# Products with the identity in TensorE's gaps ahead of the first MLP stage, and an earlier gate for one pair of loads

## The chip, the cores and the metric

The kernel runs on one NeuronCore of a Trainium2 chip. Its engines are TensorE (PE, the matmuls), VectorE (DVE), ScalarE (ACT), GpSimd (POOL) and SyncE (SP), which issues most of the DMAs. Each works through a queue of its own, in order, and waits on semaphores for the others. The metric is the device time of one execution in microseconds (us); less is better.

## The reference

Attention with normalised q and k (8 batches, 12 heads, 448 positions, head size 64), followed by an MLP over the 3584 tokens (768 to 2048 to 768):

```python
q_n = q / (norm(q) + 1e-06);  k_n = k / (norm(k) + 1e-06)
scores = matmul(q_n, k_n.T) / tau                 # tau = 0.1
attn = softmax(scores)                            # over the keys
x = matmul(attn, v)                               # heads side by side: 3584 x 768
h = x @ w_in                                      # 768 x 2048
out = (h * cos(h)) @ w_out                        # 2048 x 768
```

Inputs and output are float32; inside, the matmuls are in bfloat16.

## The kernel before, in words

**Tiling.** A *quad* is four heads of one batch: three quads make a batch, 24 quads the whole. Quads are numbered from 0; buffers rotate (`Qf`, `Kf`, `qT`, `kT` three deep, so quad 5 uses slot 2 and quad 7 slot 1, which quad 4 leaves). The 448 positions are cut in NJ = 7 slices, so `scores(7 * quad + j)` makes one slice of keys against all queries.

**One quad.** SP loads q and k (`load_qk`, L391, 448 KB each), POOL issues the load of v (L403). The squares (`square`, L436 on ScalarE or L439 on POOL) are summed on DVE (L443); `inverse` turns the sums into factors with small Ln and Exp steps on ScalarE (L461, L473) and two DVE steps (L476, L479); `scale` multiplies (L500); `transpose` turns q and k on TensorE (L522) with a copy out of PSUM (L532 on DVE, L530 on ScalarE), or, for later quads, `turn` does it by DMA (L539). `scores` is four 64x64 matmuls (L557) and one Exp of 128x896 on ScalarE, called E (L564). `spread` (L596) sums E over the keys with a matrix of ones, `attend` (L574) multiplies E with v; `invert_spread` (L609, L613) and `scale_x` (L625, DVE) finish a part of x. Where scores are made, pairs of PSUM banks alternate: score g waits until an earlier E has left its bank.

**The MLP.** For each batch c there are two stages: first `m1_part` (L677, eight pairs of 448-column sums over six 128-row slices of x and W1) with h * cos(h) behind it on ScalarE and DVE (`m1`: L690, L692, L694, L696, the result gT); then `m2` (L705, gT with W2), cut into pieces between which the scores, spreads and attends of later quads stand. Outputs leave PSUM by a DVE copy (L714) and SP's stores (L727).

**The order.** The program is written out as a list of operations (`op`), with a key each. TensorE's order is that of the keys. Up to `P.strict = False` (L954) the other engines' queues follow the keys too, which are the numbers of the operations shifted by a table, `MOVE`; behind it the Planner orders those queues when the program is built, from estimated durations and due times (`pass_`). Quads 0 to 2 are done before the first MLP stage: this is the *head*.

**Products with the identity.** `warm(n, bank)` (L803) puts n matmuls of the 128x128 identity with itself on TensorE; nothing reads what they leave. The kernel has six such groups (40, 24, 5, 8, 5 and 20).

**The gate.** POOL issues the loads of W1 (L413) and of W2 in four parts (L418, `half[2]` is parts 1 and 2, `half[3]` parts 3 and 4). The two loads of quad 5 wait until W2's third part has landed:

```python
    load_qk(5, half[3][:1])                       # L905
    ...
    load_qk(FIRST + 3, half[3])                   # L955: quad 6, after parts 3 and 4
    ...
                turn(FIRST + 1, half[3])          # L979: quad 4's transposes, likewise
```

Quad 7's loads are issued by `begin(3)` (L757), behind L954.

Of the kernel before, what the change touches and what calls it, by code (L numbers as in the profile page):

```python
# [21 lines left out]
class Planner:  # L22
# [13 lines left out]
    def __init__(self):  # L36
        self.ops = []
        self.last_write = {}
        self.readers = {}
        self.strict = False  # L40
        self.tail = {}

    def op(self, eng, dur, fn, r=(), w=(), after=(), dma=None, moves=0, mode="f", chain=None, keep=False, lead=0.0,
           packet=74, lock=False):
        o = Op()
        o.i, o.eng, o.dur, o.fn, o.dma, o.moves, o.mode, o.chain = (
            len(self.ops), eng, dur, fn, dma, moves, mode, chain)
        o.lat = self.FIRST + moves + self.LAST if dma else self.LAT[eng]
        o.behind, o.lead, o.packet, o.lock = None, lead, packet, lock
        o.key = o.i + (self.MOVE.get(o.i, 0) if self.strict else 0)  # L50
        if keep or self.strict and eng in ("act", "dve", "pool", "sp"):
            self.tail.setdefault(eng, []).append(o)
        o.reads, o.writes = tuple(r), tuple(w)
        deps = {a.i for a in after if a is not None}
        for x in o.reads:
            if x in self.last_write:
                deps.add(self.last_write[x].i)
        for x in o.writes:
            if x in self.last_write:
                deps.add(self.last_write[x].i)  # L60
            deps.update(p.i for p in self.readers.get(x, ()))
        deps.discard(o.i)
        o.deps = sorted(deps)
        for x in o.reads:
            self.readers.setdefault(x, []).append(o)
        for x in o.writes:
            self.last_write[x] = o
            self.readers[x] = []
        self.ops.append(o)
        return o  # L70

    def land(self, ring, issued, took, packet):
        s = max(issued + self.FIRST, self.ring[ring][0])
        for other, (until, theirs) in self.ring.items():
# [13 lines left out]

    def plan(self):
        for line in self.tail.values():  # L90
            line.sort(key=lambda o: o.key)
            for a, b in zip(line, line[1:]):
                b.behind = a
        self.order = self.pass_([0.0] * len(self.ops))
        return self.order
# [172 lines left out]
def bass_cosine_attention__then__act_gcu_kernel(  # L268
# [28 lines left out]
    def sb(name, shape, dt):  # L297
        return ctx.enter_context(nc.sbuf_tensor(name, shape, dt))
# [28 lines left out]
    ident = sb("ident", [128, 128], BF16)  # L327
# [4 lines left out]
    def bank(i, n=S, p0=0, p1=128):  # L332
        return PS.ap()[p0:p1, 512 * i:512 * i + n]
# [4 lines left out]
    P = Planner()  # L338
    op = P.op
    X, Y = 4, 5  # L340

    iot = ar[2].ap()[:, 0, 0:128].bitcast(I32)
    op("pool", 0.3, lambda e: e.iota(iot, [[1, 128]], base=0, channel_multiplier=-1), w=[("ar", 2)])
    op("dve", 0.25, lambda e: e.tensor_scalar(ident.ap(), iot, 0, None, ALU.is_equal), r=[("ar", 2)], w=["ident"])

    def fill_sel(e):
# [3 lines left out]
        return e.memset(sel.ap()[64:128, 16:32], 1.0)  # L350

    op("dve", 0.3, fill_sel, w=["sel"])
    op("dve", 0.1, lambda e: e.memset(ones.ap(), 1.0), w=["ones"])
    for i in range(2):
        op("dve", 0.1, lambda e, i=i: e.memset(ne.ap()[:, i, :, 1], 1e-6), w=[("eps", i)])

    mode = [None]
# [18 lines left out]
    def cut(kind, u, part):  # L376

        return [(kind, u, i) for i, (j0, j1) in enumerate(HALVES) if part[0] < j1 and j0 < part[1]]

    def whole(bk):  # L380
        return cut("B", bk, ALL[0])
# [4 lines left out]
    def load_one(qd, w, part=ALL[0], after=()):  # L386
        b, h0, s = qd // QB, 2 * (qd % QB), qd % 3
        src, dst, nm = ((q, Qf, "Qf"), (k, Kf, "Kf"))[w]
        j0, j1 = part
        ap = bass.AP(src.tensor, (b * NH + h0) * S * D + j0 * D, [[NJ * D, 128], [NH // 2 * S * D, 2], [1, (j1 - j0) * D]])  # L390
        return op("sp", 0.6, lambda e: e.dma_start(dst[s].ap()[:, :, j0:j1].rearrange("p r j d -> p r (j d)"), ap),  # L391
                  w=cut(nm, s, part), dma=(nm, s, j0), moves=0.17 * (j1 - j0), after=after)

    def load_qk(qd, after=()):
        return [load_one(qd, w, after=after) for w in range(2)]
# [98 lines left out]
    def scale(qd, w, eng="pool", part=ALL[0]):  # L494
        s, u = qd % 3, qd % 2
        j0, j1 = part
        f, n, nm = ((Qf, Qn, "Q"), (Kf, Kn, "K"))[w]
        rb = bass.AP(rr, (2 * u + w) * H + j0, [[4 * H, 128], [NJ, 2], [1, j1 - j0], [0, D]])
        return op(eng, (1.05 if eng == "dve" else 1.65) * (j1 - j0) / NJ,
                  lambda e: e.tensor_tensor(n[0].ap()[:, j0:j1].rearrange("p j r d -> p r j d"), f[s].ap()[:, :, j0:j1],  # L500
                                            rb, ALU.mult),
                  r=cut(nm + "f", s, part) + cut("rr%d" % w, u, part), w=cut(nm + "n", 0, part), lock=True)
# [44 lines left out]
    def scores(g, bs=None):  # L547
        qd, j = divmod(g, NJ)
        assert holds.get(g % NE, 0) // NJ in summed or g < NE
        holds[g % NE] = g  # L550
        u, es = qd % 3, g % NE
        bs = 2 * (g % 2) if bs is None else bs

        def mm(e):
            for r in range(2):
                for a in range(2):
                    ins = e.matmul(bank(bs + r, S, 64 * a, 64 * a + 64),  # L557
                                   kT[u].ap()[64 * r:64 * r + 64, j, a, :],
                                   qT[u].ap()[64 * r:64 * r + 64, :, a, :],
                                   start=True, stop=True)  # L560
            return ins

        op("pe", 0.2, mm, r=cut("QT", u, ALL[0]) + cut("KT", u, (j, j + 1)), w=pair(bs), mode="q")
        act("exp", 0.81, lambda e: e.activation(E[es].ap(), two(bs), ACT.Exp, bias=0.0, scale=INV_TAU),  # L564
            r=pair(bs), w=[("E", es)], chain="E")
# [52 lines left out]
    def scale_x(qd, bk=None):  # L618
        b, c0, s = qd // QB, 2 * (qd % QB), qd % 3
        if bk is None:  # L620
            sl = qd % NA
            op("dve", 1.01, lambda e: e.tensor_tensor(xT[b % 2].ap()[:, c0:c0 + 2, :], AVs[sl].ap(), ar[s].ap(), ALU.mult),
               r=[("AV", sl), ("ar", s)], w=[("x", b % 2, qd % QB)], lead=LEAD, lock=True)
            return
        op("dve", 1.01, lambda e: e.tensor_tensor(xT[b % 2].ap()[:, c0:c0 + 2, :], two(bk), ar[s].ap(), ALU.mult),  # L625
           r=pair(bk) + [("ar", s)], w=[("x", b % 2, qd % QB)])
# [146 lines left out]
    def next_pair():  # L773
        turns[0] += 1
        return 2 * (turns[0] % SLOTS)
# [9 lines left out]
    def visit(slots):  # L785
        for kind, x in slots:
# [13 lines left out]
                begin(qd)  # L800
            scores(x, next_pair())

    def warm(n, bk=0):  # L803

        def mm(e):
            for _ in range(n):
                ins = e.matmul(bank(bk, 128), ident.ap(), ident.ap(), start=True, stop=True)
            return ins

        op("pe", (0.057 if bk else 0.08) * n, mm, r=["ident"], w=whole(bk), after=[P.ops[-1]] if n < 40 and bk == 0 else ())  # L810

    P.strict = True
    warm(40)
    first = load_one(0, 0)
    for part in HALVES:
# [4 lines left out]
    half = [[], []]  # L820
# [7 lines left out]
    adds = [square(0, 1, "act", part) for part in HALVES]  # L828
    add()
    warm(24)  # L830
    adds[0]()
    adds[1]()
# [3 lines left out]
    for _ in inverse(0, 1, 2, HALVES[1]):  # L836
        pass
    scale(0, 0, "dve")
    warm(5)
    scale(0, 1, "dve", HALVES[0])  # L840
    scale(0, 1, "dve", HALVES[1])
# [60 lines left out]
    transpose(2, 1, Z + 1, HALVES[0])  # L902
    scores(12)
    scaled = scale(2, 1, "dve", HALVES[1])
    load_qk(5, half[3][:1])  # L905
    scale_x(0, X)
    scores(13)
    transpose(2, 1, Z + 1, HALVES[1])
# [156 lines left out]
```

## Time and profile before

| | us |
|---|---|
| median of 3 runs | 424.02 |
| the three runs | 423.82, 424.02, 425.92 |
| the profiled execution, time | 424.78 |
| its span, from first to last instruction | 423.0 |
| start of the first MLP stage (first L677) | 35.99 |
| start of the second MLP stage | 90.60 |
| mean granted clock of TensorE | 0.996 |

| engine | busy us | share of the span |
|---|---|---|
| PE | 408.5 | 97% |
| ACT | 308.2 | 73% |
| DVE | 268.5 | 63% |
| POOL | 201.1 | 48% |

The profile is of one execution. A busy TensorE is not TensorE at its peak, since matmuls overlap in the records: a row's length holds the time in the pipe, and successive starts show the rate. The granted clock is a share of full speed (1.00 or, where it is held back, less). "Idle before", in square brackets, is how long an engine stood still and what ended it. The chain of waits follows the work that ended last back to the start. Times in the text are from the span's start.

### The profile page before, as it was taken

How to read it: one execution, taken by the hardware profiler on the slowest of the kernel's cores; microseconds unless marked ns; L12 is line 12 of the kernel's file. 1: busy time of each engine (PE TensorE's matmuls, PEld its weight loads, DVE VectorE, ACT ScalarE, POOL GpSimd, SP SyncE). 2: the span in 40 equal slices, each digit the busy share in tenths (PEclk: the TensorE clock that was granted, in tenths of full speed). 3: DMA queues.
4: the chain of work that ended last, by engine and by line, in shares of the span. 5: the costliest groups of instructions: out<-in, count | busy, mean ns of one | idle time of the engine just before them, and what ended most of it. 6: DMA issues, size and time to landing. Idle time of an engine off the chain costs nothing.

```text
span 423.0 us, 8505 instructions
## 1 busy us (share of the span) xinstructions
PE 408.5 (97%) x3586; PEld 214.0 (51%) x3586; DVE 268.5 (63%) x335; ACT 308.2 (73%) x406; POOL 201.1 (48%) x137
## 2 busy tenths in 40 slices
PE   6889998999999999999999999999999999999996
PEld 6344454445545445445554554454554555555563
DVE  4766786888954649753896459814783137826931
ACT  5898888997888977698778848689778557605700
POOL 1476437884287796659538963269403213000000
PEclk9899999999999999999999999999999999999999
DMA  8999998997089979687949992289705624021032
GB/s 272 247 241 210 235 220 154 237 202 178 2 186 178 288 155 265 87 172 161 218 126 206 181 247 60 42 153 218 162 0 82 133 63 94 2 74 39 1 76 74
DMA packets 71127, 62.83 MB, mean 149 GB/s; under 512 B 40496, under 2 KB 66096, under 8 KB 71088
## 3 DMA queue, kind: packets, MB, share of 16 engines
q1 hardware_dynamic: 60688, 50.28, 51.9%
q0 software_dynamic: 10240, 11.80, 16.9%
q8 instruction: 28, 0.46, 0.5%
q10 hardware_dynamic: 160, 0.20, 0.1%
q14 instruction: 11, 0.09, 0.1%
HBM read 45.61 MB, written 11.01 MB: 134 GB/s over the span
## 4 chain that ended last, share of the span: by engine, by line
PE 74%; DMA 12%; DVE 4%; POOL 4%; ACT 3%; SPq 2%; issue 1%; ACTq 0%; POOLq 0%
PE PS L705 29%; PE PS L677 27%; PE PS L557 7%; PE PS L574 6%; DMA W<-in_moe_w_out_dram 6%; DMA Kf<-in_k_dram 4%; PE PS L635 3%; DMA R<-Zs 2%; ACT E L564 1%; PE PS L596 1%; SPq L656 1%; POOL xT L659 1%; POOL sqq L439 1%; DVE gT L696 1%; DVE n L443 1%
## 5 line engine op out<-in xcount | busy, mean ns | idle before, releaser
L705 PE MATMUL PS<-W,gT 128*128 128x384 bf16 x896 | 156.7, 327 | 0.0
L564 ACT ACTIVATE E<-PS 128x896 bf16<-128x896 f32 x168 | 143.2, 917 | 17.7 <-PE PS L557 16.2
L677 PE MATMUL PS<-xT,W 128*128 128x448 bf16 x768 | 147.2, 353 | 1.0 <-POOL xT L659 0.5
L705 PEld LDWEIGHTS PS<-W,gT 128*128 128x128 bf16 x896 | 83.2, 98 | 69.2 <-issue 16.2
L677 PEld LDWEIGHTS PS<-xT,W 128*128 128x128 bf16 x768 | 74.5, 98 | 71.8 <-POOL xT L659 0.9
L690 ACT ACTIVATE ar<-PS 128x896 int32<-128x896 f32 x64 | 58.1, 911 | 41.8 <-PE PS L677 41.6
L692 DVE SCALAR_TENSOR_TENSOR ar<-ar,PS 128x896 f32<-128x896 int32 x64 | 69.1, 1084 | 22.6 <-ACT ar L690 22.6
L696 DVE TENSOR_TENSOR gT<-PS,ar 128x896 bf16<-128x896 f32 x64 | 69.4, 1088 | 7.8 <-ACT ar L694 7.4
L694 ACT ACTIVATE ar<-ar 128x896 f32<-128x896 f32 x64 | 60.5, 947 | 16.6 <-DVE ar L692 16.0
L714 DVE COPY osb<-PS 128x384 f32<-128x384 f32 x56 | 31.1, 556 | 60.6 <-PE PS L705 60.1
L439 POOL TENSOR_TENSOR sqq<-Qf 128x896 bf16<-128x896 f32 x22 | 36.9, 1677 | 42.9 <-DMA Qf<-in_q_dram 22.6
L659 POOL TENSOR_TENSOR xT<-AVs,R 128x896 bf16<-128x896 f32 x18 | 37.6, 2089 | 41.4 <-DMA R<-Zs 41.2
L557 PE MATMUL PS<-qT,kT 64*64 64x448 bf16 x672 | 49.2, 362 | 4.2 <-ACT E L564 3.1
L500 POOL TENSOR_TENSOR Qn<-Qf,rr 128x896 bf16<-128x896 f32 x21 | 38.1, 1812 | 27.9 <-DVE rr L479 24.8
L439 POOL TENSOR_TENSOR sqk<-Kf 128x896 bf16<-128x896 f32 x21 | 36.8, 1754 | 17.4 <-DVE n L443 14.6
L443 DVE TENSOR_REDUCE n<-sqq 128x14 f32<-128x896 bf16 x24 | 25.7, 1072 | 24.0 <-POOL sqq L439 20.2
L583 DVE COPY AVs<-PS 128x896 f32<-128x896 f32 x21 | 22.9, 1091 | 23.5 <-PE PS L574 23.4
L574 PE MATMUL PS<-E,Vb 64*64 64x448 bf16 x672 | 37.0, 351 | 0.3 <-DVE kT L532 0.3
L557 PEld LDWEIGHTS PS<-qT,kT 64*64 64x64 bf16 x672 | 16.5, 105 | 30.2 <-issue 12.2
L500 POOL TENSOR_TENSOR Kn<-Kf,rr 128x896 bf16<-128x896 f32 x18 | 30.4, 1687 | 1.9 <-DMA kT<-Kn 1.9
L443 DVE TENSOR_REDUCE n<-sqk 128x14 f32<-128x896 bf16 (+2 forms) x25 | 26.0, 1041 | 4.6 <-POOL sqk L439 3.6
L403 POOL DMA_DIRECT2D Vb<-in_v_dram x24 | 18.1, 755 | 18.0 <-PE PS L557 12.4
(47 smaller groups left out, 180.9 us busy)
## 6 DMA issues: line engine op xcount, KB each, us to landing
Qf<-in_q_dram SPq DMA_DIRECT2D x24, 448.0 KB, 5.3
out_dram<-osb SPq DMA_DIRECT2D x54, 192.0 KB, 3.4
Kf<-in_k_dram SPq DMA_DIRECT2D x23, 448.0 KB, 6.0
R<-Zs SPq DMA_DIRECT2D x72, 112.0 KB, 3.2
Vb<-in_v_dram POOLq DMA_DIRECT2D x24, 224.0 KB, 6.6
W<-in_moe_w_in_dram POOLq DMA_DIRECT2D x4, 768.0 KB, 18.4
W<-in_moe_w_out_dram POOLq DMA_DIRECT2D x4, 768.0 KB, 24.1
qT<-Qn SPq DMA_TRANSPOSE x20, 4.0
```

Source lines behind the costliest of these rows:

```text
L439: op(eng, (1.68 if eng == "pool" else 1.05) * n, lambda e: e.tensor_tensor(dst, src, src, ALU.mult), r=cut(nm + "f", s, part), w=cut("sq" ...
L443: return op("dve", 0.07 + 0.95 * n, lambda e: e.tensor_reduce(out=n2.ap()[:, u, H * w:H * w + H] if part == ALL[0] else jr(n2, u, w, part) ...
L500: lambda e: e.tensor_tensor(n[0].ap()[:, j0:j1].rearrange("p j r d -> p r j d"), f[s].ap()[:, :, j0:j1], rb, ALU.mult),
L557: ins = e.matmul(bank(bs + r, S, 64 * a, 64 * a + 64), kT[u].ap()[64 * r:64 * r + 64, j, a, :], qT[u].ap()[64 * r:64 * r + 64, :, a, :], s ...
L564: act("exp", 0.81, lambda e: e.activation(E[es].ap(), two(bs), ACT.Exp, bias=0.0, scale=INV_TAU), r=pair(bs), w=[("E", es)], chain="E")
L574: ins = e.matmul(bank(bk + a, S, 64 * r, 64 * r + 64), Vb[vs].ap()[64 * a:64 * a + 64, r, j, :], E[es].ap()[64 * a:64 * a + 64, r, :], sta ...
L677: ins = e.matmul(bank(bk + i2), W1.ap()[:, i, 128 * nb:128 * nb + 128], xT[c % 2].ap()[:, i, :], start=(i == 0), stop=(i == NKC - 1))
L690: op("act", 0.815, lambda e: e.activation(ar[s].ap().bitcast(I32), two(bk), ACT.Identity, bias=0.25, scale=INV2PI), r=bs, w=[("ar", s)])
L692: op("dve", 1.005, lambda e: e.scalar_tensor_tensor(ar[s].ap(), ar[s].ap().bitcast(I32), -2.0 * math.pi, two(bk), ALU.mult, ALU.add), r=bs ...
L694: act("sin", 0.86, lambda e: e.activation(ar[s].ap(), ar[s].ap(), ACT.Sin, bias=GUARD * math.pi / 2.0, scale=GUARD), r=[("ar", s)], w=[("a ...
L696: op("dve", 1.01, lambda e: e.tensor_tensor(gT.ap()[:, 2 * pr:2 * pr + 2, col:col + S], two(bk), ar[s].ap(), ALU.mult), r=bs + [("ar", s)] ...
L705: ins = e.matmul(bank(bk, HW), gT.ap()[:, f, col:col + 128], W2.ap()[:, f, HW * h:HW * h + HW], start=(f == 0), stop=(f == NNB - 1))
```

## The change

Two edits.

The Planner's `op` takes an explicit key, and a table `FILL` is added. When the operation with a number in the table is made, `P.idle` first puts a group of products on TensorE, with a key just below that operation's own, so that the group stands right before it. An entry holds how many products, the PSUM bank that they write, and the mode: "f" is the 128x128 product that `warm` already makes, "q" is two 64x64 matmuls of 128 columns, both from one half of the identity's rows. There are 14 groups with 97 products: 57 full ones and 40 "q" ones. By the operation that they stand before:

| entry | products | stands before |
|---|---|---|
| 26 | 27 f | the 24 products of `warm(24)` |
| 42 | 6 f | `warm(5)` |
| 54 | 13 f | score 0 |
| 68 | 10 q | score 2 |
| 74, 77, 103 | 4, 2, 4 q | the spreads of quad 0's E 2, 3 and 6 |
| 106 | 1 q | the first attend of quad 0 |
| 129 | 7 q | quad 2's transpose of q |
| 141 | 8 q | quad 2's transpose of the last part of k |
| 147 | 4 q | score 15 |
| 230 | 8 f | quad 3's transpose of k (in the first MLP stage) |
| 236 | 2 f | the stage's fourth pair of sums |
| 302 | 1 f | a piece of the second product |

The other edit: quad 5's two loads wait for W2's second part in place of its third.

```diff
@@ Planner.__init__
+        self.count = 0
@@ Planner.op
     def op(self, eng, dur, fn, r=(), w=(), after=(), dma=None, moves=0, mode="f", chain=None, keep=False, lead=0.0,
-           packet=74, lock=False):
+           packet=74, lock=False, key=None):
+        if key is None:
+            self.count += 1
+            key = self.count - 1
+            if self.strict:
+                key += self.MOVE.get(key, 0)
+            if self.count - 1 in self.FILL:
+                self.idle(*self.FILL[self.count - 1], key - 0.01)
...
-        o.key = o.i + (self.MOVE.get(o.i, 0) if self.strict else 0)
+        o.key = key
...
+    FILL = {26: [27, 1, 'f'], 42: [6, 1, 'f'], 54: [13, 1, 'f'], 68: [10, 4, 'q'], 74: [4, 4, 'q'], 77: [2, 4, 'q'],
+            103: [4, 4, 'q'], 106: [1, 4, 'q'], 129: [7, 6, 'q'], 141: [8, 6, 'q'], 147: [4, 6, 'q'], 230: [8, 5,
+            'f'], 236: [2, 2, 'f'], 302: [1, 0, 'f']}
...
+    def products(e, n, bk, mode="f"):
+        for _ in range(n):
+            if mode == "f":
+                ins = e.matmul(bank(bk, 128), ident.ap(), ident.ap(), start=True, stop=True)
+            else:
+                p = 64 * (bk % 2)
+                for a in range(0, 128, 64):
+                    ins = e.matmul(bank(bk, 128, a, a + 64), ident.ap()[p:p + 64, 0:64], ident.ap()[p:p + 64, :],
+                                   start=True, stop=True)
+        return ins
...
+    P.idle = lambda n, bk, mode, key: op("pe", 0.06 * n, lambda e: products(e, n, bk, mode), r=["ident"], w=whole(bk),
+                                         mode=mode, key=key)
...
-    load_qk(5, half[3][:1])
+    load_qk(5, half[2][1:])
```

`warm` now calls `products`; its groups stay as they were.

More of the change, by code (lines that the diff above doesn't have):

```diff
@@ L801, in visit @@
             scores(x, next_pair())
-    def warm(n, bk=0):
[L805 to L810, printed above, removed]
+    def products(e, n, bk, mode="f"):
[8 more added lines that the diff above has]
+        return ins
+    def warm(n, bk=0):
+        op("pe", (0.057 if bk else 0.08) * n, lambda e: products(e, n, bk), r=["ident"], w=whole(bk), after=[P.ops[-1]] if n < 40 and bk == 0 else ())
+    P.idle = lambda n, bk, mode, key: op("pe", 0.06 * n, lambda e: products(e, n, bk, mode), r=["ident"], w=whole(bk),
+                                         mode=mode, key=key)
     P.strict = True
```

## The prediction

> **What bounds the kernel now.** I read the page first, then the windows, TensorE's timeline, ScalarE's waits, the chain of waits, and last the stretch in which quad 5 holds the others up.
>
> ```profile
> PE 408.5 (97%) x3586; PEld 214.0 (51%) x3586; DVE 268.5 (63%) x335; ACT 308.2 (73%) x406; POOL 201.1 (48%) x137
> ```
>
> TensorE is busy for 97% of the span, and by the windows for 40.00 of the 40 us from 90 to 130 us. What follows the second MLP stage's start at 90.60 us moves as a block: a microsecond won or lost before that is won or lost at the end. Only the head (before the first stage, at 35.99 us) and the gaps up to 90 us can give anything. The windows (stretch, TensorE busy, weight loads, DVE, ACT, POOL, granted clock, DMA share, GB/s):
>
> ```profile
> 3.91:7.33 3.42, 2.86 (x28) 2.60 (x27) 1.68 (x2) 1.60 (x3) 1.60 (x2) 1.00 1.05 361
> 7.33:10.74 3.41, 1.99 (x33) 1.72 (x31) 2.69 (x5) 3.25 (x15) 0.20 (x1) 1.00 1.12 333
> 10.74:14.15 3.41, 1.98 (x29) 1.02 (x31) 3.18 (x6) 2.59 (x4) 3.17 (x5) 1.00 1.14 306
> 14.15:17.57 3.42, 3.42 (x36) 1.41 (x29) 2.23 (x4) 2.70 (x6) 0.00 (x0) 0.50 1.11 217
> 16.74:38.21 21.47, 18.73 (x280) 9.29 (x273) 14.33 (x22) 21.10 (x30) 13.50 (x12) 0.98 1.13 226
> ```
>
> TensorE is busy for 58% of two stretches of 3.41 us, and then its clock is 0.50 for 3.42 us. The last row shows who sets the pace of the rest of the head: ScalarE, busy for 21.10 of 21.47 us.
>
> TensorE's timeline inside the slow stretch, and ScalarE's waits from 12 to 40 us (in total, times, longest):
>
> ```profile
> 15.72 0.59 PE L596 MATMUL PS<-E,ones 64*64 64x448 bf16 x4
> 16.10 0.58 PE L557 MATMUL PS<-qT,kT 64*64 64x448 bf16 x4
> ...
> 18.16 0.38 PE L557 MATMUL PS<-qT,kT 64*64 64x448 bf16 x4
> ```
>
> ```profile
> ACT E L564 <- PE PS L557: 1.4, 2, 0.7
> ACT ar L690 <- PE PS L677: 0.5, 1, 0.5
> ```
>
> A score takes 0.58 us at the low clock and 0.38 after it. ScalarE ends E(3) at 16.05 and waits until 16.74 for the score that began at 16.10. That 0.69 is one of the two score waits; the other (0.71, until 12.12) ends with a DVE copy and has nothing to do with the clock.
>
> The chain of waits (start, length, what), then the timeline from 65 to 68 us:
>
> ```profile
> 49.25 0.37 SPq L391
> ...
> 49.66 12.21 DMA Kf<-in_k_dram
> ...
> 61.94 1.69 POOL sqk L439
> ...
> 63.65 1.10 DVE n L443
> ```
>
> ```profile
> 64.77 0.23 ACT L461 ACTIVATE nrm<-n 128x28 f32<-128x28 f32 x1 [1.34 <-DVE n L443]
> 66.11 0.38 PE L557 MATMUL PS<-qT,kT 64*64 64x448 bf16 x4 [0.23 <-ACT E L564]
> 66.92 0.38 PE L557 MATMUL PS<-qT,kT 64*64 64x448 bf16 x4 [0.42 <-ACT E L564]
> 67.73 0.38 PE L557 MATMUL PS<-qT,kT 64*64 64x448 bf16 x4 [0.42 <-ACT E L564]
> ```
>
> SP issues quad 5's loads at 49.25 and 49.66, when W2's third part has landed (49.23). Its K lands at 61.87, is squared on POOL and summed on DVE, and ScalarE, whose queue has quad 5's Ln next, stands still for 1.34 us with the next scores already in PSUM. TensorE then waits three times for E, 1.07 us in all.
>
> **Part A, the products.** They are 57 full products and 40 "q" ones (two 64x64 matmuls each) in fourteen places. Full ones follow each other every 55 ns at the full clock (20 in 1.29 us) and every 106 ns before the clock rises at 7.33 us (40 in 4.45 us). A "q" product stands in no row: between 55 ns, if its two halves run side by side as four 64x64 matmuls of 448 columns do (28 in 1.45 us, about 0.21 per four), and 110 ns if they don't. I take 60, nearest to that row, and keep 110 for the range.
>
> Place by place. 27 at 5.83: 1.50/0.106 = 14 until 7.33 and 13 x 0.055 = 0.7 after it, to 8.05; the 24 products behind them end at 9.4 and the next 6 at 9.7, where the five that wait for DVE until 9.69 start anyway: nothing lost. 13 from 10.84: 0.72 us in a gap of 0.87. 10 "q" after 12.53: 0.60 (to 1.10) in a gap of 0.56, and the score behind them ends before 14.3, when ScalarE wants it: hidden either way, since it ended at 13.47. The next 11 (four places) lie where the low clock left no gap and the full one leaves TensorE waiting for E. 7 "q" in a gap of 0.45 ahead of quad 2's transposes: 0 to 0.35 late, but the scores that read them come 1.8 us later. 8 "q" before 26.97, where about 0.4 us is free (the score at 26.40 issues for 0.2): 0.1 (to 0.5) late; the score behind ends at 27.62 and is wanted at 27.93, so 0 to 0.2 lost. The following 4 are hidden by E(13). 8 full ones (0.44) come after 43.21, by when the seven transposes before them are issued, and end before 43.78; 2 more fit ahead of 44.79; one at about 64 us stands in a stretch without a gap: 0.06 on the path. I charge 0.1 in all (0.06 to 0.5).
>
> The gain: the two stretches of 58% become nearly full, and if the clock then stays at 1.00, score 4 is done at about 15.7, E(4) starts when E(3) ends (16.05), and ScalarE's 0.69 goes. Behind it all is ScalarE's own work until 37.82, then DVE's x of quad 2, then POOL and the stage; they shift together. What is late next is only the wait for the first sums, which stays. W1's first half landed by 27.5 (issues at 10.54 and 11.2, 11.3 and 16.3 us to landing, the second from a pair's median of 13.8), so it holds nothing. A = -0.65 (0 to -0.7).
>
> The Trainium skill speaks against this part: TensorE: Matmul & The Clock Gate, "Why this matters for your kernels", asks only that idle gaps stay under about 3 us, and by it this head, whose longest gap is 1.42 us, would not lose its clock, and the products would bring nothing. The 0.50 above differs from that; Part 1 of the page has a free-running window of 3.4 us, and with that the 3.42 agrees.
>
> **Part B, the gate.** W2's four parts land at 41.75, 45.5, 49.23 and 55.6 (issues at 22.15, 22.93, 23.66, 24.4, to landing 19.6, 22.6, 25.6, 31.2; the 22.6 from a pair's median of 21.1). With the second part as gate, quad 5's two loads can go at 45.5. On SP they stand beside quad 7's, which went at 45.40 and 47.03 when POOL had scaled quad 4. So I expect the order Q7, Q5, K5, K7 in place of Q7, K7, Q5, K5. The four landings were 53.6, 56.1, 58.45 and 61.87, a queue of SP's that is never empty; the order changes and the slots stay, since W2's parts and V go on beside them as before. K5 gets the third slot, 58.45, 3.4 us sooner; K7 gets the last and isn't squared before 70 us. Behind them on SP stand quad 4's two transposes, which wait for W2's fourth part until 55.6 anyway. W2's fourth part is first read at about 60.1 (the 25th of 26 matmuls, 163 ns apart, from 56.15) and has 4.4 us to spare.
>
> Then POOL squares K5 from 58.45 to 60.1 (it is idle from 47.0 to 58.55), and DVE's sum no longer waits 1.40 us for it: after the sum of Q5 (60.41) and the output copy (61.70 to 62.26) it ends at about 63.3, and ScalarE, free at 63.43, goes on with Ln, and with E at about 63.9 in place of 65.16. TensorE gets back the 1.07 and some of the drains between them, at most ScalarE's 1.34. B = -1.2 (-0.9 to -1.4).
>
> **Sum.** -0.65 - 1.2 + 0.1 = -1.75. The profiled execution took 424.78 (span 423.0, and 1.78 around it): 423.0. It lies 0.76 above the median of 424.02, about what A is worth, and runs differ by 2.1 us (423.82 to 425.92); if the slow stretch falls elsewhere in the faster runs, the median gains less of A. Between 424.02 - 1.75 = 422.3 and 423.0 I take 422.6. About 0.5%, 2.1 us, is what a measurement of this kernel can tell from no change, so the bounds are 421.9 and 426.1.
>
> **Rivals.** (1) A brings nothing: the clock falls all the same, because "q" products or another place of the window count differently, or the 0.50 had another cause than these gaps. Then -1.2 + 0.1: 422.9 from the median, 423.7 from the profiled run. For it: the stretch from 7.33 had the same 58% and no loss behind it. Against it: the 0.50 right behind a second such stretch, and 1.00 from there on, with fewer gaps. The skill's rule on gaps is on this rival's side.
>
> (2) B is hidden: K5 lands no sooner, because it now competes with W2's third and fourth parts (share over 1.1 all through 45 to 55 us). Then -0.65 + 0.1 = 424.2 from the profiled run, 423.5 from the median.
>
> (3) Slower, by DVE's queue. The queues after the head are ordered when the program is built, by estimated readiness, and a load that is estimated early can bring its sum of squares ahead of the MLP stage's last pair. DVE runs in order: if the sum of K5 stands before the last L692 (57.30), it waits for K5's square until 60.1 and ends at 61.2; the last L696, ending at 60.41 now, ends 3.9 later at 64.3, and the MLP's second product, which reads it at 61.16, waits 3.1 us, in place of B's gain: 424.02 - 0.55 + 3.1 = 426.6. It decides once the sum stands one place too early and K5's square ends later than 57.3. Against it: DVE is busy with the stage's own steps from 50.5 to 60.4 us almost without a gap, and both sums stand behind all of them now.
>
> (4) More: the 0.57 us that TensorE waits for E at 84.55 goes too, and all of ScalarE's 1.34: -0.7 - 1.34 - 0.5 = 424.02 - 2.5 = 421.5.
>
> **Chances.** The forecast 0.44 (its own range 421.8 to 423.2), (1) 0.18, (2) 0.15, (3) 0.11, (4) 0.12. Faster by over 0.5% takes (4) and a quarter of the forecast: 0.23. Slower takes (3): 0.11. The rest is 0.66. The range goes from just under (4), 421.3, to 425.4, which takes in A and B both failing with the upper charge of 0.5 and a wide run, and leaves (3) out.
>
> **What would show it.** Granted clock 1.00 from 7.33 to 36 us; no wait of ScalarE before E(4); the stage's first matmul at about 35.4; gaps of the old size at 26.97 and 43.78 filled, not passed. SP's loads of quad 5 at 45.5, K5's square on POOL by about 59; no wait in front of the Ln at 64.77's place; TensorE at the spread of quad 3 about 1.9 us before 68.64, and at the second stage at about 88.8. Wrong would be: a clock of 0.50 anywhere in the head, E(4) later than 16.3, sums of quad 5 ahead of L692 in DVE's queue, or m2 waiting for W2.

## The result, and the profile after

The changed kernel takes 422.51 us (median of 22 runs, 421.43 to 427.19) and the kernel before 425.15 (22 runs, 422.67 to 427.69). The ratio is 0.995, with a 95% interval of 0.9927 to 0.9974: 1.1 to 3.1 us faster. In a later set of runs (full_again, below) the gain did not come again: ratio 1.0009 (0.9976 to 1.0041). The profiled execution took 421.43, with a span of 419.6; it is the fastest of the 22. Of the runs of the kernel before that stand beside the experiments, six that took over 1.5% longer than the fastest are left out below, where runs are compared by their clock.

The page's first line and its chain by engine (in the profile before, DMA stood in that chain with 12%):

```profile
PE 411.3 (98%) x3723; PEld 218.8 (52%) x3723; DVE 268.4 (64%) x335; ACT 308.2 (73%) x406; POOL 201.2 (48%) x137
PE 88%; ACT 6%; DVE 2%; DMA 1%; POOL 1%; issue 0%; SPq 0%; ACTq 0%; POOLq 0%
```

The same windows as before (stretch, PE, weight loads, DVE, ACT, POOL, clock, DMA share, GB/s), and ScalarE's waits from 12 to 40 us:

```profile
7.33:10.74 3.41, 3.41 (x62) 3.24 (x58) 3.14 (x7) 2.95 (x10) 2.37 (x4) 1.00 1.12 331
10.74:14.15 3.41, 3.31 (x61) 2.00 (x60) 2.82 (x6) 2.74 (x5) 1.00 (x2) 1.00 1.18 258
14.15:17.57 3.42, 3.15 (x53) 1.63 (x51) 2.73 (x6) 3.42 (x6) 0.00 (x0) 1.00 1.10 256
```

```profile
ACT E L575 <- PE PS L568: 0.9, 1, 0.9
ACT ar L701 <- PE PS L688: 0.5, 1, 0.5
```

The two stretches of 58% are now full or nearly so (3.41 and 3.31 of 3.41 us), the clock is 1.00, and the second wait for a score is gone (the 0.9 is the one in front of E(0)). Then SP's queue, ScalarE's and TensorE's timelines around quad 5:

```profile
43.73 1.09 SPq L402 DMA_DIRECT2D Qf<-in_q_dram  x2
44.87 0.98 SPq L402 DMA_DIRECT2D Kf<-in_k_dram  x2
```

```profile
61.63 0.24 ACT L472 ACTIVATE nrm<-n 128x28 f32<-128x28 f32 x1
62.15 4.96 ACT L575 ACTIVATE E<-PS 128x896 bf16<-128x896 f32 x6
```

```profile
64.13 0.98 PE L568 MATMUL PS<-qT,kT 64*64 64x448 bf16 x12
65.05 0.66 PE L716 MATMUL PS<-W,gT 128*128 128x384 bf16 x3
65.64 1.52 PE L607 MATMUL PS<-E,ones 64*64 64x448 bf16 x28
```

Quad 7's and quad 5's loads go together. No bracket stands before the Ln at 61.63, and the scores that waited three times are one row of twelve.

Cut at three points, the two profiled executions differ like this (us):

| | before | after | difference |
|---|---|---|---|
| start of E(0) | 12.12 | 11.27 | -0.85 |
| E(0) to the first MLP stage | 23.87 | 23.04 | -0.83 |
| first to second MLP stage | 54.61 | 53.29 | -1.32 |
| second stage to the end | 332.4 | 332.0 | -0.4 |
| span | 423.0 | 419.6 | -3.4 |

The first and the last row are not what the change was made for. The first goes back to quad 0's K: before, the chain of waits has its second part landing at 7.18, and ScalarE waits 1.47 us for it; after, ScalarE squares it with no wait from about 5.7. The chain after leads from quad 0's transposes straight back through TensorE's products (start, length, what):

```profile
1.38 8.02 PE PS L817 x102
```

The experiments show how much both rows vary by themselves.

### The profile page after: what moved, and what is told of

Read it like the earlier page. It is cut to its first block, busy times and chain, and to the rows that moved or that the text cites. A ratio compares the mean times of both kernels' runs of the same rounds, so it can differ in the third digit from the quotient of the medians.

```text
span 419.6 us, 8780 instructions
## 1 busy us (share of the span) xinstructions
PE 411.3 (98%) x3723; PEld 218.8 (52%) x3723; DVE 268.4 (64%) x335; ACT 308.2 (73%) x406; POOL 201.2 (48%) x137
## 4 chain that ended last, share of the span: by engine, by line
PE 88%; ACT 6%; DVE 2%; DMA 1%; POOL 1%; issue 0%; SPq 0%; ACTq 0%; POOLq 0%
PE PS L716 34%; PE PS L688 34%; PE PS L568 8%; PE PS L585 7%; ACT E L575 4%; PE PS L646 3%; PE PS L817 2%; DMA R<-Zs 1%; PE PS L607 1%; DVE osb L725 1%; POOL xT L670 0%; DVE n L454 0%; ACT ar L701 0%; ACT ar L624 0%; ACT ar L620 0%
## 5 line engine op out<-in xcount | busy, mean ns | idle before, releaser
L701 ACT ACTIVATE ar<-PS 128x896 int32<-128x896 f32 x64 | 58.2, 911 | 42.0 <-PE PS L688 41.6
```

The lines of the kernel that those rows point to most:

```text
L701: op("act", 0.815, lambda e: e.activation(ar[s].ap().bitcast(I32), two(bk), ACT.Identity, bias=0.25, scale=INV2PI), r=bs, w=[("ar", s)])
```

## The experiments

The experiments' kernels were run 12 times each (double 11 times) and profiled once; a ratio is to runs of the kernel before on the same chip. Three chips were used, and the last column has the median of the kernel before on the same one (34 or 35 runs there, 22 for the first rows). So medians compare only where the last column agrees, and the profiles show where the time goes, each for one execution. "Stage" is the start of an MLP stage; all in us.

| kernel | E(0) | E(0) to stage 1 | stage 1 to 2 | stage 2 at | stage 2 to end | median | kernel before beside it |
|---|---|---|---|---|---|---|---|
| before | 12.12 | 23.87 | 54.61 | 90.60 | 332.4 | 425.15 | 425.15 |
| before_again | 11.16 | 23.03 | 56.87 | 91.06 | 332.64 | 425.50 | 423.57 |
| a_only | 11.27 | 23.23 | 56.26 | 90.76 | 333.44 | 424.33 | 424.69 |
| after (full) | 11.27 | 23.04 | 53.29 | 87.60 | 332.0 | 422.51 | 425.15 |
| full_again | 11.23 | 23.03 | 53.30 | 87.56 | 333.24 | 423.23 | 422.95 |
| b_only | 11.11 | 23.01 | 53.29 | 87.41 | 332.79 | 421.95 | 424.69 |
| gate_again | 12.05 | 23.57 | 53.30 | 88.92 | 332.18 | 422.19 | 422.95 |
| early | 11.81 | 23.02 | 53.30 | 88.13 | 334.57 | 423.64 | 424.69 |
| late | 11.95 | 23.02 | 53.29 | 88.26 | 333.64 | 423.45 | 424.69 |
| no_products | 11.36 | 24.33 | 53.75 | 89.44 | 331.86 | 424.21 | 422.95 |
| table_only | 11.33 | 23.03 | 53.74 | 88.10 | 333.1 | 423.19 | 423.57 |
| double | 14.05 | 24.02 | 53.29 | 91.36 | 334.94 | 427.30 | 423.57 |
| gate1 | 11.13 | 23.03 | 54.37 | 88.53 | 333.07 | 423.53 | 423.57 |
| gate4 | 11.12 | 23.02 | 55.83 | 89.97 | 334.23 | 424.83 | 422.95 |

Theory: the products are worth what a lost clock costs, the gate what quad 5's wait costs, and the two add. Rival: the gate does it all.

### One half at a time

Products without the gate (a_only):

```diff
-    load_qk(5, half[2][1:])
+    load_qk(5, half[3][:1])
```

> All 14 groups of products, quad 5's loads gated by W2's third part as before. My theory (A and B add): clock 1.00 all through the head; from E(0) to the first MLP stage 23.0 to 23.1 us (23.87 before, 23.04 after); from the first to the second stage 54.6 as before (53.29 after), with the wait in front of quad 5's Ln still about 1.3 us; in all 0.7 us faster than before. Rival 1 (the products bring nothing, all comes from the gate): E(0) to stage 23.8, time as before. Rival 2 (the two need each other, since W2 is issued earlier): stage to stage under 54.

Measured: 424.33 against 424.69 before (35 runs), ratio 1.0 (0.9965 to 1.0035). The head was quick, though E(0) to the stage is 23.23 and not 23.0 to 23.1 (ScalarE waited 0.22 us for a late spread). Nothing was left of it at the second stage: 90.76 against 90.60 before. ScalarE, POOL and TensorE:

```profile
64.94 0.23 ACT L470 ACTIVATE nrm<-n 128x28 f32<-128x28 f32 x1 [2.98 <-DVE n L452]
```

```profile
59.74 1.68 POOL L448 TENSOR_TENSOR sqq<-Qf 128x896 bf16<-128x896 f32 x1 [14.22 <-DMA Qf<-in_q_dram]
62.11 1.68 POOL L448 TENSOR_TENSOR sqk<-Kf 128x896 bf16<-128x896 f32 x1 [0.69 <-DMA Kf<-in_k_dram]
```

```profile
63.06 1.15 PE L714 MATMUL PS<-W,gT 128*128 128x384 bf16 x6 [2.18 <-DVE osb L723]
```

K of quad 5 is squared at 62.11, as before (61.94), though the head ended 1.5 us sooner: SP could issue quad 5's loads only at 53.19 here (49.25 before), since W2's third part landed 4 us later in this execution. The wait before Ln grew from 1.34 to 2.98, and DVE's sum of Q5, which stood ahead of an output copy in its queue and waited for POOL, held up that copy and TensorE behind it (2.18). The gain of the head was given back at quad 5. The time is rival 1's; the reason is in none of the three expectations.

The gate without the table (b_only; the same kernel again as gate_again on another chip):

```diff
-    FILL = {26: [27, 1, 'f'], 42: [6, 1, 'f'], ...}
+    FILL = {}
```

> No products of the table, quad 5's loads gated by W2's second part. My theory: the clock falls to 0.50 for one window in the head, E(0) to the first stage 23.8 to 23.9, stage to stage 53.3, no wait of ScalarE in front of quad 5's Ln; 1.3 us faster than before. Rival 1: nearly all of the 2.1 us. Rival 2 (the gate alone does not help): stage to stage 54.6 and time as before.

> The gate alone (W2's second part), the table of products empty, on the same chip as the full change. 'Gate alone': 421.9 to 422.6 us and stage to stage 53.3. 'Products too': 422.8 or more, with a clock of 0.996 or less in a third of the runs.

> The changed kernel once more, to stand beside the next one on the same chip. Theory 'gate alone' (in a head that keeps its clock the products bring nothing): median within 0.5 us of the kernel with the gate alone, E(0) to the first stage 23.0 us in both. Theory 'products too': 0.5 us or more faster than the gate alone, by runs in which the gate alone loses its clock.

Measured: b_only 421.95 against 424.69, ratio 0.9951 (0.9921 to 0.9982). On another chip, gate_again 422.19 and full_again 423.23 against 422.95 before; ratios 0.9984 (0.9960 to 1.0009) and 1.0009 (0.9976 to 1.0041). The gate without the table is nowhere behind the full change, and the full change is level there with the kernel before. My expectations fared badly: full_again is 1.04 us behind the gate alone, where one theory had them within 0.5 and the other had it ahead; gate_again has the time of 'gate alone' and, in 4 of 12 runs, the clock of 0.996 or less of 'products too'. In b_only's profile the clock, which I expected to fall, held without the table, and E(0) to the stage is 23.01. In gate_again's it did not, as these rows show (with ScalarE's waits from 12 to 40 us behind them):

```profile
10.74:14.15 3.41, 2.33 (x23) 1.14 (x22) 3.12 (x5) 2.32 (x3) 2.93 (x5) 0.67 1.15 263
14.15:17.57 3.42, 3.42 (x48) 1.71 (x46) 2.27 (x5) 3.07 (x6) 0.00 (x0) 0.83 1.09 240
```

```profile
ACT E L573 <- PE PS L566: 1.0, 2, 0.7
```

So a lost clock costs 0.56 there (23.57) and 0.84 in the profile before, and in the other four profiles without the table but with the kernel's own products (b_only, before_again, gate1, gate4) it costs nothing, since the clock was not lost (23.01 to 23.03).

What sets the two groups apart is visible ahead of E(0): TensorE's wait for quad 0's scaled q in the profile before, in gate_again and in b_only.

```profile
9.75 0.45 PE L807 MATMUL PS<-ident 128*128 128x128 bf16 x5 [1.42 <-DVE Qn L500]
9.68 0.45 PE L815 MATMUL PS<-ident 128*128 128x128 bf16 x5 [1.81 <-DVE Qn L509]
8.74 0.45 PE L815 MATMUL PS<-ident 128*128 128x128 bf16 x5 [0.80 <-DVE Qn L509]
```

In the first two, which lost the clock, the second part of quad 0's K was late (ScalarE waited 1.47 and 1.44 us for it). In the four that kept it, that wait is at most 0.34 us, and TensorE's is about 0.8 as in b_only. So the table may pay in executions whose first loads are late. Two profiles against four suggest it; no run tests it.

### The kernel before, once more

> The kernel before, for a second profile of it. If the wait for quad 5 belongs to the gate at the third part, stage to stage is 54 to 57 us whatever the head took, and the start of the second stage lies at 90.2 to 91.0 us even when the head is a microsecond shorter. If the 1.3 us was peculiar to the one profile, 53.3 to 53.5.

Measured: 425.5 for this copy and 423.57 for the kernel before beside it, the same program on the same chip: ratio 1.0036 (0.9996 to 1.0076). Differences of 0.4% between two kernels of this table are therefore within what one kernel shows against itself. The profile bears on the gate, but only in part:

```profile
63.62 0.23 ACT L461 ACTIVATE nrm<-n 128x28 f32<-128x28 f32 x1 [1.98 <-DVE n L443]
```

```profile
65.00:70.00 5.00, 4.15 (x39) 1.59 (x43) 2.25 (x3) 3.94 (x5) 5.00 (x3) 0.71 0.70 109
```

```profile
91.06 1.11 PE L677 MATMUL PS<-xT,W 128*128 128x448 bf16 x5
```

The head kept its clock without the table, and the first stage began at 34.19, 1.8 us before that of the first profile. The second began at 91.06, 0.5 us later. The wait for quad 5 was longer, and behind it the clock fell (0.71 from 65 to 70 us): there the spread of quad 3 takes 2.83 us, and 1.52 in the kernel after. Of the 2.26 us by which stage 1 to 2 is longer than in the first profile, 0.65 lie ahead of the first score that quad 5 held up (64.96 here, 66.11 there) and 1.61 behind it, where the clock fell. So the larger part is the clock's. I expected 90.2 to 91.0 for the start of stage 2; the direction held, the size missed by 0.06. With the third part as gate, stage 2 starts at 90.60, 90.76 and 91.06 in the three profiles, quick head or not; with the second part, at 87.4 to 91.4, and there it follows the head.

These three profiles don't stand for most executions with the old gate. A start at 90.60, the shortest rest in the table (331.86) and the least time around a span (1.75) make 424.2 us; 64 of the 98 runs of the kernel before on the three chips took less, and none like them is profiled. A window of 3.42 us at 0.50 brings a run's mean clock to 0.996, which both profiles of this kernel have. Of 110 runs (the 98 and this copy's 12), the 26 at 0.996 or less have a median of 425.54 us, the other 84 one of 422.96. In those 84 either the wait for quad 5 was shorter or the rest went faster; which, no profile shows.

### Do products keep the clock?

> Only the first two groups of products (27 and 6, ahead of 9.75 us), with the new gate. They fill the stretch from 5.8 to 9.7 and leave the stretch from 10.7 to 14.2 at 58% busy. If one stretch of that kind is enough to lose the clock, it falls to 0.50 for 3.4 us at about 14 and E(0) to stage is 23.8. If it needs two in a row, the clock holds and E(0) to stage is 23.1 to 23.2.

> All groups but the first two, with the new gate. They fill what comes after 10.8 us and leave the stretch from 7.3 to 10.7 as before. If that stretch alone can lose the clock, it falls to 0.50 somewhere between 10 and 14.5 us, and E(0) to stage is over 23.3; if the loss before came from the stretch from 10.7 to 14.2, the clock holds and E(0) to stage is 23.0 to 23.1.

Both have the new gate and one end of the table (entries 26 and 42; or all the others). Measured: 23.02 in each, clock 1.00; 423.64 and 423.45, ratios 0.998 (0.9948 to 1.0011) and 0.9966 (0.9938 to 0.9993). By the expectations, "two in a row" and "not that stretch alone" would both fit, but neither run settles it. b_only holds its clock with neither end, so one profile with early's end decides nothing. And late did not leave the stretch from 7.33 to 10.74 half empty: the kernel's own 29 products took 3.27 us there (1.51 and 0.45 in b_only), and TensorE was busy for all of its 3.41 us. This stays open.

The stronger test takes the kernel's own products away too (with the table empty), and then puts the table back:

```diff
     def warm(n, bk=0):
+        if n < 40:                                # no_products
+            P.count += 1
+            return
...
+        if n < 40:                                # table_only: the table's groups stay
+            if P.count in P.FILL:
+                P.idle(*P.FILL[P.count], P.count - 0.01)
+            P.count += 1
+            return
```

> The new gate, no products of the table, and the kernel's own five later groups of products (24, 5, 8, 5 and 20) left out too, so that after 5.8 us TensorE makes only the real work of the head. If products keep the clock, it falls to 0.50 for one window or more between 7 and 18 us, E(0) to the first stage is 23.7 or more and the time 0.7 to 2 us above the gate alone. If the head does not need them at all, clock 1.00 and 23.0 us.

> As the kernel without products (new gate, the five later groups of the kernel before left out), but with the table's 14 groups in. If products in these gaps keep the clock, the clock is 1.00 in the head, E(0) to the first stage is 23.0 to 23.2 us (24.33 without any) and fewer than 3 of 12 runs have a mean clock under 0.990 (7 of 12 without any). If the clock goes by something else, 23.7 or more and many runs under 0.990.

no_products, windows; then table_only:

```profile
7.33:10.74 3.41, 1.37 (x15) 1.11 (x15) 3.24 (x7) 2.98 (x10) 1.97 (x3) 0.57 1.12 333
10.74:14.15 3.41, 2.98 (x27) 0.91 (x27) 2.36 (x4) 2.30 (x5) 1.40 (x3) 0.50 1.18 271
14.15:17.57 3.42, 3.01 (x30) 1.37 (x27) 2.14 (x4) 3.16 (x5) 0.00 (x0) 0.50 1.09 257
```

```profile
7.33:10.74 3.41, 1.69 (x24) 1.35 (x24) 3.12 (x6) 3.27 (x12) 0.69 (x2) 1.00 1.11 338
10.74:14.15 3.41, 2.77 (x55) 1.60 (x55) 2.82 (x6) 2.68 (x5) 2.68 (x4) 1.00 1.14 319
```

Without products after the first 40 the clock is 0.50 for some 10 us and the head takes 24.33; 9 of 12 runs have a mean clock of 0.992 or less. With the table back it is 23.03, and 1 of 12 is that low. So products do keep the clock here. It is a harder case than the kernel before, as without any products TensorE waits 3.54 us for quad 0's q; in the kernel before its own products fill a part of that, and the clock is lost in a smaller share of the runs. Medians: 424.21 (ratio 1.0023, 0.9997 to 1.005) and 423.19 (0.9984, 0.9952 to 1.0015). Both have 53.7 from stage to stage, 0.45 more than the others with this gate, with TensorE waiting 0.5 us for a DVE copy; leaving the groups out also changes what the Planner sees, and I did not follow that further.

### What the products cost without cover

```diff
-    FILL = {26: [27, 1, 'f'], 42: [6, 1, 'f'], 54: [13, 1, 'f'], 68: [10, 4, 'q'], ...}
+    FILL = {26: [54, 1, 'f'], 42: [12, 1, 'f'], 54: [26, 1, 'f'], 68: [20, 4, 'q'], ...}
```

> The full change with every group of the table twice as long (194 products). The added 97 cost 5.3 us of TensorE if nothing hides them. By my reckoning of the gaps those ahead of score 2 (20 q in 0.6 us), of quad 2's transposes (14 and 16 q) and of quad 3's k transpose (16 f in 0.5 us) run over: E(0) to the first stage 23.3 to 24.5 us, and stage to stage 53.7 to 54.0. If TensorE has slack everywhere ahead of the stage (ScalarE sets the pace), 23.0 to 23.1 still.

Measured: 427.3, ratio 1.0089 (1.0056 to 1.0123). ScalarE's waits from 11 to 92 us:

```profile
ACT E L573 <- PE PS L566: 4.2, 4, 3.3
```

E(0) starts at 14.05, 2.8 us after the full change's, and E(0) to the stage is 24.02: 3.8 us lost of some 5.4 added, most of it ahead of E(0), a place that I had not named. E(0) to the stage is inside the 23.3 to 24.5 that I expected. Stage to stage is 53.29, unchanged, where I expected 0.4 to 0.7 more. Twice the table does not fit.

### The gate earlier and later

```diff
-    load_qk(5, half[2][1:])
+    load_qk(5, half[2][:1])                       # gate1
+    load_qk(5, half[3][1:])                       # gate4
```

The table is empty in both.

> No products of the table, quad 5's loads gated by W2's first part. K of quad 5 then lands no later than with the second part (57 us), and ScalarE already has no wait in front of its Ln there: stage to stage 53.3 again and 421.9 to 422.6 us. If each earlier slot still pays, stage to stage is under 53. If the loads now hold up W2, the second product waits for W2's third or fourth part and stage to stage is over 53.8.

> No products of the table; quad 5's loads wait for W2's fourth part. If the time from stage to stage is set by when quad 5's K lands (third part: 61.9, second: 57.2), the loads go at about 55 us, K lands at 62 to 66, and stage to stage is 55 to 59 us (54.6 with the third part, 53.3 with the second): 1 to 5 us slower than the gate at the second part plus its 1.3. If something else held the third-part kernel, stage to stage stays at 54.6 and the time at 424.5.

gate1: 423.53, ratio 1.001 (0.9978 to 1.0043), and stage to stage 54.37, a length that only the third expectation allowed, and not for its reason: no wait for W2 stands in front of the second product. DVE's timeline says why:

```profile
49.14 1.09 DVE L452 TENSOR_REDUCE n<-sqq 128x14 f32<-128x896 bf16 x1 [1.47 <-POOL sqq L448]
50.15 1.08 DVE L701 SCALAR_TENSOR_TENSOR ar<-ar,PS 128x896 f32<-128x896 int32 x1
```

The sum of Q5 now stands inside the MLP stage, waits 1.47 us for POOL, and the stage's own L701 waits behind it: 1.1 us. gate4: 424.83, ratio 1.003 (0.9999 to 1.006), 55.83 from stage to stage, inside the 55 to 59 that I expected, but not for that reason alone. K5 was squared at 59.97, ahead of the 62 to 66 that I expected and sooner than with the third part (its load went at 54.12, when W2 had landed, and took under 6 us, not 12), and ScalarE had no wait before Ln; the order of the queues had changed, and TensorE's longest wait came late:

```profile
86.68 0.38 PE L566 MATMUL PS<-qT,kT 64*64 64x448 bf16 x4 [1.49 <-ACT E L573]
```

Of the four gates the second part has the shortest way from stage to stage in these profiles, and the landing time of K5 is not all that a gate moves.

## Why the prediction was right

The forecast was 422.6, in a range of 421.3 to 425.4; 422.51 was measured, and the largest chance was on a change within 0.5% (the ratio's middle is 0.5% itself). Both mechanisms were seen where the prediction put them: the clock held in the head, and the wait in front of quad 5's Ln went. That their sum met the time is in part luck. Point by point:

- **The gate.** The order Q7, Q5, K5, K7 and the third slot came as worked out. W2's second part landed at about 44.4, K5 at 57.2 (44.87 and 12.3 to landing; 58.45 was forecast), squared at 57.19. The wait before Ln is gone. The step was -1.2, at most -1.34; it measured -1.32 between the two profiles.
- **The products.** Behind E(0) the groups fit, as read. Ahead of it they don't quite: "nothing lost" for the first two groups rested on DVE being done at 9.69, which came of the late K. In the profile after, the scaled q is there at 8.65 and quad 0's transposes start at 9.24, behind the products (9.03 in b_only, without the table). So the products, and no longer K, stand in the chain there. E(0) starts at 11.27 and 11.23 in the two profiles of the full change, and at 11.11 to 11.16 in the four that kept the clock without the table: about 0.1 us lost, as much as was charged for other places. A "q" product takes about 56 ns (20 of its matmuls in a row of 0.75 us, of which 0.22 is one matmul's own length: 28 ns from start to start), 60 in the prediction. The step for the clock was -0.65; the profiles show -0.83, but only between an execution that lost its clock and one that did not.
- **The step that failed is the sum.** It added the two parts as if the head's gain would "shift together" to the second stage in either kernel. In the profiles with the old gate it does not (stage 2 at 90.60, 90.76, 91.06): quad 5's loads wait for W2's third part, which landed at 49.23, 53.18 (a_only) and 48.34 (before_again), while the heads of the last two were 1.5 and 1.8 us quicker. In a_only the late landing takes back all that the head won. In before_again the longer wait takes 0.65, and a clock lost behind it 1.61. So the wait that I read as 1.34 us is not a fixed size: from stage 1 to 2 the old gate costs 1.3, 3.0 and 3.6 more than the 53.3 of the new one, the last with the lost clock in it. Behind the old gate the products are then worth nothing, and behind the new one 0 to 0.8. What they are worth in the executions that were not profiled stays open.
- **Which median.** I chose between two bases, 424.02 and the profiled 424.78. Over 22 runs the kernel before has 425.15; three runs were too few for a choice of 0.7. From there the medians differ by 2.64 us (2.1 by the ratio), where the sum had 1.75. The base was too low and the gain too small, and the level came out right; this is luck. So is the set of runs: full_again's ratio, 1.0009 (0.9976 to 1.0041), would not have borne out any gain.
- **Rival 1** (the products bring nothing) holds for the median: the gate without the table is level with the full change or ahead of it (421.95 and 422.19 against 422.51 and 423.23; of these only 422.19 and 423.23 share a chip). Mean clocks of 0.996 or less came in 26 of 110 runs of the kernel before, 6 of 34 of the full change and 5 of 24 of the gate alone: no clear difference. The six runs of the full change have a median of 425.63 us and the other 28 one of 422.53, a larger difference than the 0.56 to 0.84 that a lost clock costs in the head. Where the clock fell in them no profile shows; it stays open.
- **The rule of the Trainium skill on gaps**, TensorE: Matmul & The Clock Gate, "Why this matters for your kernels", would have had no lost clock in this head. The runs differ: 0.50 with no gap over 1.42 us (before), and again with none over 1.81 (gate_again). The rule's consequence, that the table is worth little, came out all the same, for another reason.
- **Rival 3** (a sum in DVE's queue ahead of the stage's steps) did not happen with the second part, and did with the first: 1.1 us, not the 3.1 that I priced for a later place. **Rivals 2 and 4** did not: K5 landed sooner, and TensorE's wait for E before the last spread (0.57 at 84.55 before) is 0.58 at 81.55 after.

A version that was nowhere behind the full change is the gate alone: ratio 0.9951 (0.9921 to 0.9982) on one chip and 0.9984 (0.9960 to 1.0009) on another, without 97 products. That it beats the full change is not shown.

## What to carry to other kernels

Before two gains along one path are added, look for a wait between them that ends with something neither of them moves, here a DMA gate: ahead of it, time that is won can be given back (all of 1.5 us in a_only, 0.65 of 1.8 in before_again), and the gate's own worth changes with it. Cut the profile at a few points of the program and compare the pieces over several executions: from E(0) to the first stage nine profiles that kept the clock agree within 0.03 us (a_only is 0.2 longer), where the whole varies by over 5. And take a second profile of the kernel before, of an execution near the median: one execution can show a loss (here the clock) that most don't have.

## What was not expected of the hardware

From the second stage to the end, a part that no kernel here changes in substance, took 331.86 to 334.94 us. In the two longest of the kernels with the second-part gate and a table of single length, TensorE waits for a part of x from POOL for 1.4 us (early, 334.57) and 1.8 (late, 333.64), and 0.3 in the kernel after (332.0). E(0) started between 11.11 and 12.12 us (double left out): late where the second part of quad 0's K was late (before, gate_again) or where products stood in front of quad 0's transposes (late, whose own 29 took 3.27 us). The first spread is larger than the change, the second about half of it.

The low clock stays on in a stretch that is itself busy: in no_products it was 0.50 through two stretches in which TensorE was busy for 2.98 and 3.01 of 3.4 us. What share keeps it or loses it can't be read from these windows, as stretches of 1.99 and 1.98 of 3.41 (before) and one of 1.59 (gate_again) came before a loss, and one of 1.69 (table_only) and 1.75 (b_only) did not.
